# Row sums of an attention block moved from TensorE to VectorE, with three shared FFN banks in PSUM

## Chip, cores and metric

The kernel runs on one core of one Trainium2 chip. The metric is the device time of one execution in microseconds (us), median of several executions. An execution is slow when it lies over 1.5% above the fastest of its kernel. Differences of about 1 us between two kernels are near the noise: the 95% interval of a ratio is 0.2 to 0.7% wide on each side. The profile comes from one extra execution of each kernel. Its span is about 1.7 us shorter than the device time (before: 274.5 against 276.1 us).

## The reference

Block-sparse attention, then a multiplicative feed-forward network (FFN) without an activation:

```python
# q, k, v: (4 batches, 8 heads, 768 positions, 64), float32
scores = q @ k.T / 8                     # per batch and head
mask = same block or a neighbour, or first/last block on either side,
       or one of 3 sampled blocks        # blocks of 32; the same mask for every head
attn = exp(scores) / sum(exp(scores))    # over the unmasked keys
x = (attn @ v) as (3072 tokens, 512)
out = ((x @ w1) * (x @ w2)) @ w3 @ w_out # 512 -> 1024 -> 1024 -> 512, float32
```

## The kernel before

Everything on the chip is bfloat16 with float32 sums in PSUM. Scores are computed transposed (keys on partitions, queries along the free dimension), so that the weights `e` can be the moving operand of the value product. A sum over keys is then a sum over partitions, and TensorE makes it, with a matrix of ones as the stationary operand. `w3 @ w_out` is folded into one matrix `wf` on the chip, because nothing stands between the two.

The work: 4 batches x 3 query tiles of 256 x 2 sets of four heads = 24 groups. Each group has 3 pairs of key chunks (6 x 128 keys). One score unit is two heads of one pair: 4 score matmuls, one exp on ScalarE (1024 elements a partition), one mask multiplication on VectorE. One pair of four heads then goes through the value matmuls:

```python
def values(b, t, Q, kp):                 # one pair of key chunks, four heads
    def emit(eng):
        if kp == 0:
            acc["o"] = ps_o.tile([128, 512], F32, tag="o", name="o")
            acc["d"] = ps_o.tile([128, QT], F32, tag="d", name="d")   # own bank
        ...
        for k2 in range(2):
            kc = 2 * kp + k2
            first, last = kc == 0, kc == C - 1
            for part in range(3):        # parts 0, 1: two halves of v; part 2: ones
                for g in range(4):
                    ...
                    if part == 2:
                        nc.tensor.matmul(d[rows, :], lhsT=ones, rhs=rhs, start=first, ...)
                    else:
                        nc.tensor.matmul(o[rows, part * QT:(part + 1) * QT], lhsT=vn[...], rhs=rhs, ...)
```

Four matmuls with 32 output rows each (`g`) run side by side in the array: in the trace of this kernel they start 3 to 4 ns apart, and the next set of four 0.109 us after the set before it. So there are 1152 value matmuls and 576 matmuls with ones. After the third pair ScalarE makes 1/d as exp(-ln d), and VectorE writes `x = o * (1/d)`.

The kernel lays out PSUM in eight banks: four for two score tiles, one for `o`, one for `d`, two (`ps_f`) for everything else: FFN (`pa`, `pb`, `po`), the folding of the weights (`w3p`, `wp`) and the mask building.

The order of instructions is fixed when the program is built. A list scheduler ("planner") has an estimated duration for each operation. It places attention units (modes "qk", "pv") and takes FFN pieces (mode "f") as filler between them.

```python
# pick_pe, shortened
if rv is not None and rv <= near:                      # a value burst is ready
    op = self.pv[0]
    whole = all(o.ready() is not None and o.ready() <= rv + 0.3 for o in ...)
    if op.kp or (whole and self.mode == "qk") or rf is None or rf > near:
        return rv, self.pv
if rf is not None and rf <= near and self.due > 0.3:   # FFN owed: SHARE per score unit
    return rf, self.fill
...
```

The softmax here doesn't subtract the row's maximum and nothing guards it: scores larger than these inputs give would overflow.

## Time and profile before

| | before |
|---|---|
| device time | 276.1 us |
| PE, DVE, ACT busy | 97, 68, 66% of the span |
| PE's part of the chain of waits | 91% |
| last attention work (last `x`) ends | 243 us |
| last score matmul at half speed | about 20 us |

The page's busy table and the first two lines of the chain of waits (who the last instruction was waiting for, followed back to the start):

```profile
span 274.5 us, 7499 instructions
PE 265.9 (97%) x3228; PEld 135.1 (49%) x3228; DVE 186.5 (68%) x299; ACT 180.0 (66%) x241; POOL 63.0 (23%) x100
PE 91%; ACT 3%; DVE 3%; POOL 1%; issue 1%; POOLq 0%; ACTq 0%
PE pa L597 16%; PE pb L614 16%; PE po L635 16%; PE s L466 15%; PE o L508 13%; PE d L505 6%; PE wp L578 4%; ACT e L473 3%; PE tp L375 3%; PE mp L446 1%; DVE e L477 1%; PE w3p L561 1%; POOL A L257 0%; DVE wf_sb L284 0%; DVE qkt L284 0%
```

The sums (`d`, L505) are 6% of the chain. Groups of instructions by line and shape (lines that are left out are marked ...); after the first bar stand busy time and mean ns of one:

```profile
L477 DVE TENSOR_TENSOR e<-e,mask 128x1024 bf16<-128x1024 bf16 x144 | 98.5, 688 | 47.8 <-ACT e L473 46.6
...
L505 PE MATMUL d<-e,ones 128*32 128x256 bf16 x576 | 41.9, 277 | 0.0
```

Busy time of matmuls counts overlap once per group but not between groups, so 41.9 us is not what they cost. The start times say more. From the timeline of PE, columns start, length, line, tile, shape and count:

```profile
142.88 1.04 PE L597 MATMUL pa<-x,w_sb 128*128 128x512 bf16 x4
143.76 1.03 PE L614 MATMUL pb<-x,w_sb 128*128 128x512 bf16 x4
144.70 1.02 PE L597 MATMUL pa<-x,w_sb 128*128 128x512 bf16 x4
145.66 0.40 PE L508 MATMUL o<-e,vn 128*32 128x256 bf16 x8
145.88 0.28 PE L505 MATMUL d<-e,ones 128*32 128x256 bf16 x4
...
147.74 0.61 PE L466 MATMUL s<-qkt 64*128 64x256 bf16 x8
148.28 1.04 PE L614 MATMUL pb<-x,w_sb 128*128 128x512 bf16 x4
```

One burst of 72 value and sum matmuls takes 2.08 us (145.66 to 147.74), of which a third are sums.

```profile
1.21 3.17 PE L278 MATMUL warm<-warm_sb 128*128 128x512 bf16 x7 [1.21 <-DVE warm_sb L239]
...
13.15 0.61 PE L466 MATMUL s<-qkt 64*128 64x256 bf16 x4
...
22.44 0.39 PE L466 MATMUL s<-qkt 64*128 64x256 bf16 x4
```

Four score matmuls take 0.61 us at 13 us and 0.39 us at 22 us. The records of one engine overlap (`pa` matmuls last 0.38 us and start 0.22 us apart), so the distance from start to start is the better measure: matmuls of 512 columns start 0.43 us apart at the beginning (`warm`) and 0.22 us apart later (`pa`). So the array runs at half its later speed for the first 20 us, although PE is busy most of the time (9.5 of the 10 us from 10 to 20 us). The page's row of the granted clock shows 9 (90% or more) for these slices too, so only the matmuls tell: the trace holds no record of the clock before 20.8 us, and the row counts time without a record as full speed.

### The profile page before, as it was taken

The page shows a single profiled execution, that of the slowest core. Times are in us where ns is not written, and L with a number is a line of the kernel's source. Part 1 is how long each engine was busy: PE and PEld are TensorE (multiplying, and loading weights), DVE is VectorE, ACT ScalarE, POOL GpSimd, SP SyncE. Part 2 cuts the span into 40 slices and gives each one's busy share as a digit, 9 for nine tenths or more (in the row PEclk, how much of TensorE's full clock was granted, in tenths as well). Part 3 has the DMA queues.
Part 4 walks back from the last instruction along what each step waited for, and adds up shares of the span by engine and source line. Part 5 has one row for each costly group of instructions (what it writes and reads, how often), then busy time and mean ns, then how long its engine had stood idle before and what let it go on. Part 6 is the DMA issues. An engine that isn't in the chain of part 4 may idle for free.

```text
span 274.5 us, 7499 instructions
## 1 busy us (share of the span) xinstructions
PE 265.9 (97%) x3228; PEld 135.1 (49%) x3228; DVE 186.5 (68%) x299; ACT 180.0 (66%) x241; POOL 63.0 (23%) x100
## 2 busy tenths in 40 slices
PE   6999999899999999999999999999999999999994
PEld 2445555445554545545455544554554555444441
DVE  5576657767688677677755868666767656756752
ACT  4667669865557797595996679978868968520000
POOL 8635568944290000038510000000000000000000
PEclk9999999999999999999999999999999999999999
DMA  7999999999695051069993000300002100002003
GB/s 224 170 206 206 204 205 203 188 156 146 83 133 38 13 163 41 0 80 128 178 173 122 2 0 2 117 38 2 2 0 79 58 25 2 2 38 115 2 21 132
DMA packets 53734, 25.39 MB, mean 93 GB/s; under 512 B 39237, under 2 KB 48709, under 8 KB 53701
## 3 DMA queue, kind: packets, MB, share of 16 engines
q0 software_dynamic: 36176, 13.90, 43.2%
q1 hardware_dynamic: 17344, 10.88, 15.7%
q8 instruction: 25, 0.41, 0.6%
q10 hardware_dynamic: 180, 0.13, 0.1%
q14 instruction: 9, 0.07, 0.1%
HBM read 29.36 MB, written 6.29 MB: 130 GB/s over the span
## 4 chain that ended last, share of the span: by engine, by line
PE 91%; ACT 3%; DVE 3%; POOL 1%; issue 1%; POOLq 0%; ACTq 0%
PE pa L597 16%; PE pb L614 16%; PE po L635 16%; PE s L466 15%; PE o L508 13%; PE d L505 6%; PE wp L578 4%; ACT e L473 3%; PE tp L375 3%; PE mp L446 1%; DVE e L477 1%; PE w3p L561 1%; POOL A L257 0%; DVE wf_sb L284 0%; DVE qkt L284 0%
## 5 line engine op out<-in xcount | busy, mean ns | idle before, releaser
L473 ACT ACTIVATE e<-s 128x1024 bf16<-128x1024 f32 x144 | 141.4, 1028 | 31.4 <-PE s L466 31.3
L477 DVE TENSOR_TENSOR e<-e,mask 128x1024 bf16<-128x1024 bf16 x144 | 98.5, 688 | 47.8 <-ACT e L473 46.6
L508 PE MATMUL o<-e,vn 128*32 128x256 bf16 x1152 | 52.4, 278 | 0.8 <-DVE x L541 0.5
L466 PE MATMUL s<-qkt 64*128 64x256 bf16 x576 | 48.9, 279 | 1.4 <-ACT e L473 1.1
L597 PE MATMUL pa<-x,w_sb 128*128 128x512 bf16 x192 | 49.5, 380 | 0.0
L614 PE MATMUL pb<-x,w_sb 128*128 128x512 bf16 x192 | 49.4, 379 | 0.0
L635 PE MATMUL po<-wf_sb,h 128*128 128x512 bf16 x192 | 44.7, 380 | 0.0
L505 PE MATMUL d<-e,ones 128*32 128x256 bf16 x576 | 41.9, 277 | 0.0
L466 PEld LDWEIGHTS <-qkt 64*128 64x128 bf16 x576 | 22.1, 95 | 31.4 <-issue 26.8
L508 PEld LDWEIGHTS <-vn 128*32 128x32 bf16 x1152 | 27.8, 97 | 16.7 <-issue 15.5
L620 DVE TENSOR_TENSOR h<-pb,a 128x512 bf16<-128x512 f32 x48 | 33.0, 687 | 3.6 <-PE pb L614 2.6
L614 PEld LDWEIGHTS <-w_sb 128*128 128x128 bf16 x192 | 17.8, 97 | 23.5 <-issue 4.8
L635 PEld LDWEIGHTS <-h 128*128 128x128 bf16 x192 | 17.3, 98 | 22.3 <-issue 3.6
L597 PEld LDWEIGHTS <-w_sb 128*128 128x128 bf16 x192 | 16.3, 97 | 22.1 <-issue 6.5
L317 POOL DMA_DIRECT2D vn<-in_v_dram x16 | 11.5, 722 | 48.4 <-PE d L505 46.8
L284 DVE CAST a<-pa 128x512 bf16<-128x512 f32 x27 | 18.6, 688 | 5.6 <-PE pa L597 5.6
L532 ACT ACTIVATE ln<-d 128x256 f32<-128x256 f32 x24 | 9.2, 385 | 17.4 <-PE d L505 17.2
L643 ACT COPY ob<-po 128x256 f32<-128x256 f32 x1 | 0.4, 372 | 28.4 <-PE po L635 28.4
L541 DVE TENSOR_TENSOR x<-o,rec 128x512 bf16<-128x512 f32 x24 | 16.4, 685 | 2.6 <-ACT rec L536 2.5
L505 PEld LDWEIGHTS <-ones 128*32 128x32 bf16 x576 | 16.4, 98 | 0.5
L578 PE MATMUL wp<-wo_sb,w3t_sb 128*128 128x512 bf16 x64 | 16.5, 381 | 0.0
L284 ACT CAST a<-pa 128x512 bf16<-128x512 f32 x21 | 12.2, 582 | 5.7 <-PE pa L597 5.7
(56 smaller groups left out, 156.3 us busy)
## 6 DMA issues: line engine op xcount, KB each, us to landing
out_dram<-ob SPq DMA_DIRECT2D x23, 256.0 KB, 2.0
vn<-in_v_dram POOLq DMA_DIRECT2D x16, 192.0 KB, 5.9
w_sb<-in_moe_w_dram POOLq DMA_DIRECT2D x8, 256.0 KB, 10.2
w_sb<-in_moe_w_dram POOLq DMA_DIRECT2D x16, 128.0 KB, 5.4
nt<-in_q_dram POOLq DMA_DIRECT2D x16, 96.0 KB, 4.6
nt<-in_k_dram POOLq DMA_DIRECT2D x16, 96.0 KB, 4.8
qn<-in_q_dram POOLq DMA_DIRECT2D x6, 192.0 KB, 8.4
kn<-in_k_dram POOLq DMA_DIRECT2D x6, 192.0 KB, 8.4
```

Source lines behind the costliest of these rows:

```text
L284: (nc.scalar.copy if eng == "ACT" else nc.vector.tensor_copy)(dst, src)
L466: nc.tensor.matmul(s[:, h, k2 * QT:(k2 + 1) * QT], lhsT=qk[64 * h:64 * h + 64, 1, kc * 128:(kc + 1) * 128], rhs=qk[64 * h:64 * h + 64, 0, ...
L473: nc.scalar.activation(e, box["s"], AF.Exp, scale=1.0 / 8.0)
L477: nc.vector.tensor_tensor(e, e, mask[:, t, kp:kp + 1, :].to_broadcast((128, 2, 512)), op=ALU.mult)
L505: nc.tensor.matmul(d[rows, :], lhsT=ones, rhs=rhs, start=first, stop=last, skip_group_check=True)
L508: nc.tensor.matmul(o[rows, part * QT:(part + 1) * QT], lhsT=vn[b, 2 * Q + i][:, h, kc, 32 * part:32 * part + 32], rhs=rhs, start=first and ...
L541: nc.vector.tensor_tensor(X[i][:, 2 * Q:2 * Q + 2, half * QT:(half + 1) * QT], box["o"].rearrange("p (s n) -> p s n", s=2), box["rec"].to_ ...
L578: nc.tensor.matmul(box["p"], lhsT=w3t_sb[:, j, i * 128:(i + 1) * 128], rhs=wo_sb[:, j, :], start=j == 0, stop=j == NF - 1)
L597: nc.tensor.matmul(p, lhsT=w1_sb[:, c, f * 128:(f + 1) * 128], rhs=X[i][:, c, :], start=c == 0, stop=c == 3)
L614: nc.tensor.matmul(p, lhsT=w2_sb[:, c, f * 128:(f + 1) * 128], rhs=X[i][:, c, :], start=c == 0, stop=c == 3)
L620: nc.vector.tensor_tensor(box["h"][:, f, :], box["pb", f], box["a", f], op=ALU.mult)
L635: nc.tensor.matmul(box["o", n], lhsT=box["h"][:, f, n * 128:(n + 1) * 128], rhs=wf_sb[:, f, :], start=f == 0, stop=f == NF - 1)
```

## The change

The intent: `e` of one group is summed over its three pairs by VectorE (two elementwise adds of 2048 elements a partition), and TensorE multiplies only that sum with ones. That leaves 8 in place of 24 matmuls for each group. To make room on VectorE, the masks of four heads become one operation, which also skips the query columns that belong to the first or last block, where the mask is one everywhere (960 x 2 in place of 1024 x 2 elements). The sums no longer hold a bank of their own; the FFN pool gets a third bank, and sums take one of the three. Further: seven buffers of `e` for four heads in place of thirteen for two; transposes of q and k in two halves through the FFN pool, which ScalarE may copy out too; four w3 buffers in place of eight; new numbers in the planner; dummy matmuls in the planned gaps of TensorE before the first value product.

```diff
-    ps_f = pool("ps_f", 2, space=PSUM)
+    ps_f = pool("ps_f", 3, space=PSUM)
...
-    warm(7)
+    def warm(gap):
+        for _ in range(int(gap / 0.22)):
+            nc.tensor.matmul(spare[:, :256], lhsT=warm_sb[:, :128], rhs=warm_sb[:, :256], ...)
+    warm(3.1)
...  # in the planner, before the first value product: self.warm(start - self.free["PE"] - 0.2)
-    SHARE = 0.6
+    SHARE = 0.58
+    COLD = 6.0          # matmuls planned before 6 us count double
...
-            nc.vector.tensor_tensor(e, e, mask[:, t, kp:kp + 1, :].to_broadcast((128, 2, 512)),
-                                    op=ALU.mult)
+            e = E[key].rearrange("p g (c n) -> p g c n", c=4)[:, :, :, 4:124]
+            m = mask[:, t, kp:kp + 1, :].rearrange("p o (c n) -> p o c n", c=4)[:, :, :, 4:124]
+            nc.vector.tensor_tensor(e, e, m.to_broadcast((128, 4, 4, 120)), op=ALU.mult)
...
+        def add1(eng):
+            box["sum"] = dpool.tile([128, 4, 512], BF16, tag="sum", name="sum")
+            nc.vector.tensor_tensor(box["sum"], E[es[0]], E[es[1]], op=ALU.add)
+        def add2(eng):
+            nc.vector.tensor_tensor(box["sum"], box["sum"], E[es[2]], op=ALU.add)
...
+        def sums(eng):
+            d = acc["d"] = ps_f.tile([128, 512], F32, tag="f", name="d")
+            for k2 in range(2):
+                for g in range(4):
+                    nc.tensor.matmul(d[32 * g:32 * g + 32, :QT], lhsT=ones,
+                                     rhs=box["sum"][:, g, k2 * QT:(k2 + 1) * QT], start=k2 == 0, ...)
...
```

More of the change, by code (lines that the diff above doesn't have):

```diff
@@ L46, in __init__ @@
         self.mode, self.lat = mode, lat
+        self.after = 0.0
         self.end = None
@@ L54, in ready @@
                 return None
-            at = max(at, e)
+            at = max(at, e + self.after)
         for slots, _ in self.takes:
@@ L67, with __init__ @@
     PATIENCE = 0.2
-    SHARE = 0.6
-    def __init__(self, free):
+    SHARE = 0.58
+    COLD = 6.0
+    def __init__(self, free, warm):
         self.free = dict(free)
+        self.warm = warm
         self.side = {e: [] for e in self.free if e != "PE"}
@@ L84, in run_op @@
         if eng == "PE":
+            if op.mode == "pv":
+                self.warm = None
+            if self.warm:
+                self.warm(start - self.free[eng] - 0.2)
             if op.mode != self.mode:
@@ L94, in run_op @@
             slots.taken.append(hold)
-        self.free[eng] = start + op.dur
-        op.end = start + op.dur + op.lat
+        dur = op.dur
+        if eng == "PE" and start < self.COLD:
+            dur *= 2
+        self.free[eng] = start + dur
+        op.end = start + dur + op.lat
         op.emit(eng)
@@ L117, in pick_pe @@
             whole = all(o.ready() is not None and o.ready() <= rv + 0.3
-                        for o in list(self.pv)[1:3 - op.kp])
-            if op.kp or (whole and self.mode == "qk") or rf is None or rf > near:
+                        for o in list(self.pv)[1:1 + op.rest])
+            if not op.first or (whole and self.mode == "qk") or rf is None or rf > near:
                 return rv, self.pv
@@ L154, in go @@
             start, _, eng, op, q = best
+            start = max(self.free[eng], op.ready())
             if eng == "PE":
@@ L199 @@
     wts = pool("wts", 1)
+    w3pool = pool("w3pool", 4)
     nat = pool("nat", 4)
@@ L202 @@
     qkt = pool("qkt", 8)
-    epool = pool("epool", 13)
+    NE = 7
+    epool = pool("epool", NE)
+    dpool = pool("dpool", 2)
     small = pool("small", 2)
@@ L210 @@
     ps_o = pool("ps_o", 1, space=PSUM)
-    ps_f = pool("ps_f", 2, space=PSUM)
-    S_SLOTS, F_SLOTS, O_SLOTS = Slots(2), Slots(2), Slots(1)
-    E_SLOTS, X_SLOTS, A_SLOTS, H_SLOTS, T_SLOTS = Slots(13), Slots(3), Slots(4), Slots(2), Slots(8)
+    ps_f = pool("ps_f", 3, space=PSUM)
+    S_SLOTS, F_SLOTS, O_SLOTS = Slots(2), Slots(3), Slots(1)
+    E_SLOTS, D_SLOTS = Slots(NE), Slots(2)
+    X_SLOTS, A_SLOTS, H_SLOTS, T_SLOTS = Slots(3), Slots(4), Slots(2), Slots(8)
+    N_SLOTS, W_SLOTS = Slots(4), Slots(4)
     order = tc.manual_schedule(
@@ L272 @@
                                        in1=A, op0=ALU.is_equal, op1=ALU.max)
-    def warm(n):
-        w = ps_f.tile([128, 512], F32, tag="f", name="warm")
-        for _ in range(n):
-            nc.tensor.matmul(w, lhsT=warm_sb[:, :128], rhs=warm_sb, start=True, stop=True)
-    warm(7)
-    plan = Planner({"PE": 4.3, "ACT": 2.6, "DVE": 4.3, "POOL": 3.4, "SP": 3.0})
+    spare = ps_o.tile([128, 512], F32, tag="o", name="spare")
+    def warm(gap):
+        for _ in range(int(gap / 0.22)):
+            nc.tensor.matmul(spare[:, :256], lhsT=warm_sb[:, :128], rhs=warm_sb[:, :256],
+                             start=True, stop=True)
+    warm(3.1)
+    plan = Planner({"PE": 4.3, "ACT": 2.6, "DVE": 4.3, "POOL": 3.4, "SP": 3.0}, warm)
     def copy(eng, dst, src):
@@ L292, in load @@
     def load(emit, nbytes, deps=()):
-        op = plan.add(Op("POOL", 0.75, None, deps))
+        op = plan.add(Op("POOL", 0.75, None))
+        op.deps = deps
         def go(eng):
@@ L302 @@
     qn, kn, vn, landed = {}, {}, {}, {}
-    nat_users = {"q": [], "k": [], "v": [], "nt": []}
+    nat_users = {"q": [], "k": [], "v": []}
     def nat_slot(tag, n):
@@ L327 @@
     w2_sb = wts.tile([128, 4, d_ff], BF16, tag="w2")
-    w3_sb = wts.tile([128, NF, d_ff], BF16, tag="w3")
     w3t_sb = wts.tile([128, NF, d_ff], BF16, tag="w3t")
@@ L341, in load_w12, with emit @@
         return op
-    w3_in = {}
+    w3_in, w3_sb, w3_hold = {}, {}, {}
     def load_w3(lo, hi):
         for i in range(lo, hi):
-            w3_in[i] = load(lambda i=i: nc.gpsimd.dma_start(
-                out=w3_sb[:, i, :], in_=moe_w3[128 * i:128 * i + 128, :]), 128 * d_ff * 4)
+            def emit(i=i):
+                w3_sb[i] = w3pool.tile([128, d_ff], BF16, tag="w3", name="w3")
+                nc.gpsimd.dma_start(out=w3_sb[i], in_=moe_w3[128 * i:128 * i + 128, :])
+            w3_in[i] = load(emit, 128 * d_ff * 4)
+            w3_hold[i] = Hold()
+            w3_in[i].takes.append((W_SLOTS, w3_hold[i]))
     QK, QK_at, QK_hold = {}, {}, {}
@@ L367, in transposes, with emit @@
     def transposes(b, pr):
-        box = {}
-        def emit(eng):
-            tp = box["p"] = ps_s.tile([128, 2, 1024], BF16, tag="s", name="tp")
-            for x, src in ((0, qn[b, pr]), (1, kn[b, pr])):
+        hold = qk_hold(b, pr)
+        ops = []
+        for x, (tag, nat_of) in enumerate((("q", qn), ("k", kn))):
+            box = {}
+            def emit(eng, x=x, nat_of=nat_of, box=box):
+                tp = box["p"] = ps_f.tile([128, 1024], BF16, tag="f", name="tp")
                 for c in range(C):
@@ L374, in emit @@
                     for h in range(2):
-                        nc.tensor.transpose(tp[64 * h:64 * h + 64, x, c * 128:(c + 1) * 128],
-                                            src[:, h, c, :], ident)
-        ins = [landed["q", b, pr], landed["k", b, pr]]
-        hold = Hold()
-        op = Op("PE", 0.66, emit, ins, [(S_SLOTS, hold)], "t", lat=0.2)
-        for d in ins:
-            d.users.append(op)
-        def out_(eng):
-            t = QK[b, pr] = qkt.tile([128, 2, S], BF16, tag="qkt", name="qkt")
-            copy(eng, t, box["p"][:, :, :S])
@@ L386, in transposes, with out_ @@
-        hold.frees = QK_at[b, pr] = plan.add(Op("DVE", 0.9, out_, [op],
-                                                [(T_SLOTS, qk_hold(b, pr))]))
-        return op
+                        nc.tensor.transpose(tp[64 * h:64 * h + 64, c * 128:(c + 1) * 128],
+                                            nat_of[b, pr][:, h, c, :], ident)
+            src = landed[tag, b, pr]
+            op = Op("PE", 0.33, emit, [src], [(F_SLOTS, Hold())], "t", lat=0.2)
+            src.users.append(op)
+            def out_(eng, x=x, box=box):
+                if x == 0:
+                    QK[b, pr] = qkt.tile([128, 2, S], BF16, tag="qkt", name="qkt")
+                copy(eng, QK[b, pr][:, x, :], box["p"][:, :S])
@@ L390 @@
+            at = plan.add(Op(("DVE", "ACT"), 0.5, out_, [op] + ([QK_at[b, pr]] if x else []),
+                             [] if x else [(T_SLOTS, hold)]))
+            op.takes[0][1].frees = QK_at[b, pr] = at
+            ops.append(op)
+        return ops
+    MARGIN = 3.0
     qd, kd = (x.rearrange("b h (p c) d -> b p c h d", c=C) for x in (q, k))
     def turned(b, pr):
-        ns = {}
-        ops = []
-        deps = []
+        ns, ops, holds = {}, [], []
         for x, src in enumerate((qd, kd)):
-            mine, was = nat_slot("nt", 4)
+            hold = Hold()
+            holds.append(hold)
@@ L403, in emit @@
                     nc.gpsimd.dma_start(out=n[:, :, h, :], in_=src[b][:, :, 2 * pr + h, :])
-            ops.append(load(emit, 2 * 128 * 2 * C * D * 4, was))
-            deps.append(mine)
+            op = load(emit, 2 * 128 * 2 * C * D * 4)
+            op.takes.append((N_SLOTS, hold))
+            ops.append(op)
         load_one(b, pr, "v")
         def turn(eng):
+            dma_at[0] += 4.0
             t = QK[b, pr] = qkt.tile([128, 2, S], BF16, tag="qkt", name="qkt")
@@ L412, in turn @@
                                             in_=ns[x].rearrange("p c h d -> p (c h d)"))
-        op = QK_at[b, pr] = plan.add(Op("SP", 0.9, turn, ops + [QK_at[b - 1, o] for o in range(4)],
-                                        [(T_SLOTS, qk_hold(b, pr))], lat=4.0))
-        for mine in deps:
-            mine.append(op)
+        op = QK_at[b, pr] = plan.add(Op("SP", 2.5, turn,
+                                        ops + [QK_at[b - 1, o] for o in range(4)],
+                                        [(T_SLOTS, qk_hold(b, pr))], lat=2.5))
+        op.after = MARGIN
+        for hold in holds:
+            hold.frees = op
     hot2 = hot.rearrange("e c p -> e (c p)")
@@ L451, in build_mask @@
         return op
-    E, E_at, E_hold = {}, {}, {}
+    E, E_at, E_hold, exps = {}, {}, {}, {}
     def scores(b, t, Q, kp, i):
         box = {}
-        key = (b, t, Q, kp, i)
+        key = (b, t, Q, kp)
         def emit(eng):
@@ L471, in exp @@
         def exp(eng):
-            e = E[key] = epool.tile([128, 2, 512], BF16, tag="e", name="e")
-            nc.scalar.activation(e, box["s"], AF.Exp, scale=1.0 / 8.0)
+            if key not in E:
+                E[key] = epool.tile([128, 4, 512], BF16, tag="e", name="e")
+            nc.scalar.activation(E[key][:, 2 * i:2 * i + 2, :], box["s"], AF.Exp, scale=1.0 / 8.0)
         def keep(eng):
-            e = E[key]
-            nc.vector.tensor_tensor(e, e, mask[:, t, kp:kp + 1, :].to_broadcast((128, 2, 512)),
-                                    op=ALU.mult)
+            e = E[key].rearrange("p g (c n) -> p g c n", c=4)[:, :, :, 4:124]
+            m = mask[:, t, kp:kp + 1, :].rearrange("p o (c n) -> p o c n", c=4)[:, :, :, 4:124]
+            nc.vector.tensor_tensor(e, e, m.to_broadcast((128, 4, 4, 120)), op=ALU.mult)
         hold = Hold()
-        E_hold[key] = Hold()
         op = Op("PE", 0.22, emit, [QK_at[b, 2 * Q + i]], [(S_SLOTS, hold)], "qk", lat=0.2)
-        hold.frees = plan.add(Op("ACT", 0.97, exp, [op], [(E_SLOTS, E_hold[key])]))
-        E_at[key] = plan.add(Op("DVE", 0.62, keep, [hold.frees, mask_at[t, kp]]))
+        takes = []
+        if key not in exps:
+            E_hold[key] = Hold()
+            takes.append((E_SLOTS, E_hold[key]))
+        hold.frees = plan.add(Op("ACT", 0.97, exp, [op] + exps.get(key, []), takes))
+        exps.setdefault(key, []).append(hold.frees)
+        if len(exps[key]) == 2:
+            E_at[key] = plan.add(Op("DVE", 1.09, keep, exps[key] + [mask_at[t, kp]]))
         QK_hold[b, 2 * Q + i].frees = op
@@ L487, with values, product, emit @@
     acc = {}
-    def values(b, t, Q, kp):
-        def emit(eng):
-            if kp == 0:
-                acc["o"] = ps_o.tile([128, 512], F32, tag="o", name="o")
-                acc["d"] = ps_o.tile([128, QT], F32, tag="d", name="d")
-            o, d = acc["o"], acc["d"]
-            es = [E.pop((b, t, Q, kp, i)) for i in range(2)]
-            for k2 in range(2):
-                kc = 2 * kp + k2
-                first, last = kc == 0, kc == C - 1
-                for part in range(3):
-                    for g in range(4):
-                        i, h = divmod(g, 2)
-                        rhs = es[i][:, h, k2 * QT:(k2 + 1) * QT]
-                        rows = slice(32 * g, 32 * g + 32)
-                        if part == 2:
-                            nc.tensor.matmul(d[rows, :], lhsT=ones, rhs=rhs, start=first,
-                                             stop=last, skip_group_check=True)
-                        else:
-                            nc.tensor.matmul(o[rows, part * QT:(part + 1) * QT],
+    def values(b, t, Q):
+        box = {}
+        es = [(b, t, Q, kp) for kp in range(3)]
+        ins = [landed["v", b, 2 * Q + i] for i in range(2)]
+        d_hold = Hold()
+        def add1(eng):
[3 more added lines that the diff above has]
+            nc.vector.tensor_tensor(box["sum"], box["sum"], E[es[2]], op=ALU.add)
+        sum1 = plan.add(Op("DVE", 1.16, add1, [E_at[es[0]], E_at[es[1]]], [(D_SLOTS, d_hold)]))
+        sum2 = plan.add(Op("DVE", 1.16, add2, [sum1, E_at[es[2]]]))
+        def product(kp):
+            def emit(eng):
+                if kp == 0:
+                    acc["o"] = ps_o.tile([128, 512], F32, tag="o", name="o")
+                e = E[es[kp]]
+                for k2 in range(2):
+                    kc = 2 * kp + k2
+                    for part in range(2):
+                        for g in range(4):
+                            i, h = divmod(g, 2)
+                            nc.tensor.matmul(acc["o"][32 * g:32 * g + 32, part * QT:(part + 1) * QT],
@@ L509, in emit @@
                                              lhsT=vn[b, 2 * Q + i][:, h, kc,
                                                                    32 * part:32 * part + 32],
-                                             rhs=rhs, start=first and part == 0, stop=last,
+                                             rhs=e[:, g, k2 * QT:(k2 + 1) * QT],
+                                             start=kc == 0 and part == 0, stop=kc == C - 1,
                                              skip_group_check=True)
-        ins = [landed["v", b, 2 * Q + i] for i in range(2)]
@@ L514, in values @@
-        op = Op("PE", 0.65, emit, [E_at[b, t, Q, kp, i] for i in range(2)] + ins,
-                [(O_SLOTS, Hold())] if kp == 0 else (), "pv", lat=0.2)
-        for i in range(2):
-            E_hold[b, t, Q, kp, i].frees = op
-        for d in ins:
-            d.users.append(op)
-        op.kp = kp
-        return op
+            return emit
+        def sums(eng):
+            d = acc["d"] = ps_f.tile([128, 512], F32, tag="f", name="d")
+            for k2 in range(2):
+                for g in range(4):
+                    nc.tensor.matmul(d[32 * g:32 * g + 32, :QT], lhsT=ones,
+                                     rhs=box["sum"][:, g, k2 * QT:(k2 + 1) * QT], start=k2 == 0,
+                                     stop=k2 == 1, skip_group_check=True)
@@ new lines, in values @@
+        o_hold = Hold()
+        ops = []
+        for kp in range(3):
+            op = Op("PE", 0.43, product(kp), [E_at[es[kp]]] + ins,
+                    [(O_SLOTS, o_hold)] if kp == 0 else (), "pv", lat=0.2)
+            op.rest, op.first = 3 - kp, kp == 0
+            ops.append(op)
+        E_hold[es[0]].frees, E_hold[es[1]].frees = ops[0], ops[1]
+        E_hold[es[2]].frees = ops[2]
+        for d in ins:
+            d.users.append(ops[2])
+        f_hold = Hold()
+        op = Op("PE", 0.22, sums, [sum2], [(F_SLOTS, f_hold)], "pv", lat=0.2)
@@ L523, with normalize @@
+        op.rest, op.first = 0, False
+        ops.append(op)
+        d_hold.frees = op
+        plan.pv.extend(ops)
+        normalize(b, t, Q, o_hold, f_hold, op)
     X, X_at, X_hold = {}, {}, {}
-    def normalize(b, t, Q, first, last):
+    def normalize(b, t, Q, o_hold, f_hold, last):
         i, half = divmod(b * NT + t, 2)
@@ L531, in ln_ @@
             box["ln"] = small.tile([128, QT], F32, tag="ln", name="ln")
-            nc.scalar.activation(box["ln"], box["d"], AF.Ln)
+            nc.scalar.activation(box["ln"], box["d"][:, :QT], AF.Ln)
         def rec_(eng):
@@ L544, in x_ @@
                 box["rec"].to_broadcast((128, 2, QT)), op=ALU.mult)
-        ln = plan.add(Op("ACT", 0.34, ln_, [last]))
+        ln = f_hold.frees = plan.add(Op("ACT", 0.34, ln_, [last]))
         rec = plan.add(Op("ACT", 0.36, rec_, [ln]))
@@ L550, in normalize @@
             takes = [(X_SLOTS, X_hold[i])]
-        x_op = first.takes[0][1].frees = plan.add(Op("DVE", 0.62, x_, [rec], takes))
+        x_op = o_hold.frees = plan.add(Op("DVE", 0.62, x_, [rec], takes))
         X_at.setdefault(i, []).append(x_op)
@@ L561, in emit @@
                 nc.tensor.transpose(tp[:, j, :],
-                                    w3_sb[:, i, (4 * jh + j) * 128:(4 * jh + j + 1) * 128], ident)
+                                    w3_sb[i][:, (4 * jh + j) * 128:(4 * jh + j + 1) * 128], ident)
         op, hold = f_op(0.23, emit, [w3_in[i]])
+        w3_hold[i].frees = op
         hold.frees = either(0.42, lambda eng: copy(
@@ L720 @@
                 turned(b + 1, pr)
-        plan.qk.extend(at.get(n, ()))
+        for ops in at.get(n, ()):
+            plan.qk.extend(ops)
         plan.qk.append(scores(*g, i))
-        if n % 2 == 1 or n == 2:
-            pass
-    for n, g in enumerate(groups):
-        b, t, Q, kp = g
-        plan.pv.append(values(*g))
-        if kp == 2:
-            normalize(b, t, Q, plan.pv[-3], plan.pv[-1])
-            while nx < NX and len(X_at.get(nx, ())) == 4:
-                ffn(nx)
-                nx += 1
+    for b, t, Q, kp in groups[::3]:
+        values(b, t, Q)
+        while nx < NX and len(X_at.get(nx, ())) == 4:
+            ffn(nx)
+            nx += 1
     plan.go()
```

## The prediction

> **What bounds the kernel now.** TensorE. The page's busy table gives PE 97% of the 274.5 us span, DVE 68%, ACT 66%; the chain of waits is 91% PE. Busy by stretches: PE idle is 8.6 us in all, 4.9 us of it before 60 us and 3.7 us at the end, after the last matmul. Attention ends at 242 us; then PE runs FFN alone.
>
> A second loss hides in "busy": the timeline shows every matmul at half speed until about 20.4 us (four score matmuls 0.61 us, later 0.39). [...]
>
> **Removed.** Row sums: 576 matmuls (L505) become 192. In the timeline a whole burst of 72 matmuls runs from 102.28 to 104.36 us: 0.029 us each, 0.116 per four. The 384 removed are worth 384 x 0.027 to 0.029 = 10.4 to 11.1 us. The chain of waits has L505 at 5.7% of the span, so all of it is on PE's path.
>
> **Startup.** Dummy matmuls fill PE's gaps until the first value product. If that frees the clock at about 6 us instead of 20.4, the 13 us of cold work becomes 6.5. But exp, mask copies and loads then set the pace, so I count 3.5 us.
>
> **Added.** DVE: 144 masks (0.69 us long, 0.61 from start to start when back to back) become 72 of 1920 elements, and 48 adds of 2048 elements come in. [...] DVE goes from 186 to about 220 us busy, as some copies move to ACT (180 to about 190). From 10 to 232 us both would be near 86 to 88% (now about 75%). That leaves less slack: I allow 2.5 us of new PE stalls on s, o and f banks. The longer chain add, sum, ln, exp, x (about 2.5 us more) matters little with 10 us per group.
>
> **Moved.** Sums and transposes take FFN banks, now three. Halving the w3 buffers makes the in-order load queue wait for w3 transposes, which could delay w1, w2 and the first FFN tile (first pa at 64.7 us).
>
> **Sum.** 276.05 - 10.6 (sums) - 3.5 (clock) + 2.5 (stalls) = 264.4 us, rounded to 264; range 257 to 270.5. Faster by over 2%: 0.87; within 2%: 0.10; slower: 0.03.
>
> **What would show it.** Row-sum matmuls 192, their busy near 14 us; adds near 1.2 us, masks near 1.15 us; DVE busy 215 to 230 us; PE still 94 to 97% busy and over 85% of the chain; score matmuls at full speed from 6 to 10 us; attention ending near 230 us, first pa near 60 us.
>
> **What would make it wrong.** [...] DVE and ACT together too full, so that PE waits for masks and bank copies (PE below 92%: 268 to 275). Loads late after the w3 wait, leaving PE idle at 40 to 65 us. The other way: a startup gain of all 6.5 us and no new stalls: 257 to 259.

The sum came to 276.05 - 10.6 - 3.5 + 2.5 = 264.4 us. Two steps stand as the author's guesses, which the trace of before did not show: that dummy matmuls end the stretch at half speed (behind the 3.5 us), and the durations that gave 45 us more of masks and adds (behind "about 220 us" of VectorE, together with the copies that move to ACT).

## The result

The changed kernel takes 262.24 us (median of 4; 261.74 to 262.64), the kernel before 276.1 us: a ratio of 0.951 (95% interval 0.947 to 0.955), 13.9 us less. Ratios here are the mean time of one kernel's fast runs over that of the other's of the same rounds, so not quite the ratio of the quoted medians. The predicted 264.0 us was close, but the sum behind it was not right in every term, as the experiments show.

The page after:

```profile
span 260.9 us, 6636 instructions
PE 248.4 (95%) x2819; PEld 127.6 (49%) x2852; DVE 212.3 (81%) x250; ACT 198.8 (76%) x274; POOL 62.7 (24%) x100
PE 86%; DVE 5%; ACT 3%; DMA 2%; issue 2%; SPq 1%
PE pb L678 17%; PE po L699 16%; PE pa L661 16%; PE s L496 14%; PE o L552 13%; PE wp L642 4%; DMA raw<-in_k_dram 2%; DVE e L509 2%; PE d L564 2%; PE tp L399 2%; ACT e L504 2%; PE mp L476 1%; DVE x L604 1%; PE w3p L624 1%; SPq L251 1%
```

TensorE is still the bound; the sums fell from 6% to 2% of the chain. VectorE went up by 26 us, ScalarE by 19 us (copies that VectorE no longer had time for). Of the matmuls 33 records are missing (2852 weight loads, 2819 matmuls), so sums over matmuls below come from traces without gaps. The groups that answer to those of before:

```profile
L509 DVE TENSOR_TENSOR e<-e,mask 128x1920 bf16<-128x1920 bf16 x72 | 82.9, 1154 | 16.7 <-ACT e L504 15.7
...
L535 DVE TENSOR_TENSOR sum<-e 128x2048 bf16<-128x2048 bf16 x24 | 29.3, 1222 | 0.7
L538 DVE TENSOR_TENSOR sum<-sum,e 128x2048 bf16<-128x2048 bf16 x24 | 29.3, 1222 | 0.5
...
L564 PE MATMUL d<-sum,ones 128*32 128x256 bf16 x192 | 9.5, 274 | 0.4 <-DVE sum L538 0.4
```

The adds took 1222 ns for 2048 elements. The strided 120-element runs of the mask kept the same rate: 1154 ns for 1920. Against the 688 ns for 1024 elements before, both take 0.52 ns more for each element more.

A burst, in the timeline of PE:

```profile
150.15 0.61 PE L496 MATMUL s<-qkt 64*128 64x256 bf16 x8
150.69 1.50 PE L552 MATMUL o<-e,vn 128*32 128x256 bf16 x48
152.01 0.39 PE L564 MATMUL d<-sum,ones 128*32 128x256 bf16 x8
152.33 1.04 PE L661 MATMUL pa<-x,w_sb 128*128 128x512 bf16 x3
```

It takes 1.64 us (150.69 to 152.33) for a whole group, against 2.08 us: 0.44 us, times 24 groups 10.6 us. And the start:

```profile
1.21 3.17 PE L295 MATMUL spare<-warm_sb 128*128 128x256 bf16 x14 [1.21 <-DVE warm_sb L255]
...
13.66 0.61 PE L496 MATMUL s<-qkt 64*128 64x256 bf16 x4
...
14.52 0.39 PE L295 MATMUL spare<-warm_sb 128*128 128x256 bf16 x1
...
19.28 1.03 PE L496 MATMUL s<-qkt 64*128 64x256 bf16 x8
```

Only one dummy matmul was placed after the opening ones, and score matmuls are as slow at 19 us as before (eight in 1.03 us). So the 3.5 us that the prediction booked for an earlier clock cannot have come from there in this execution. Something else paid.

### The profile page after: what moved, and what is told of

Read it like the earlier page. It is cut to its first block, busy times and chain, and to the rows that moved or that the text cites. A ratio compares the mean times of both kernels' runs of the same rounds, so it can differ in the third digit from the quotient of the medians.

```text
span 260.9 us, 6636 instructions
## 1 busy us (share of the span) xinstructions
PE 248.4 (95%) x2819; PEld 127.6 (49%) x2852; DVE 212.3 (81%) x250; ACT 198.8 (76%) x274; POOL 62.7 (24%) x100
## 4 chain that ended last, share of the span: by engine, by line
PE 86%; DVE 5%; ACT 3%; DMA 2%; issue 2%; SPq 1%
PE pb L678 17%; PE po L699 16%; PE pa L661 16%; PE s L496 14%; PE o L552 13%; PE wp L642 4%; DMA raw<-in_k_dram 2%; DVE e L509 2%; PE d L564 2%; PE tp L399 2%; ACT e L504 2%; PE mp L476 1%; DVE x L604 1%; PE w3p L624 1%; SPq L251 1%
## 5 line engine op out<-in xcount | busy, mean ns | idle before, releaser
L509 DVE TENSOR_TENSOR e<-e,mask 128x1920 bf16<-128x1920 bf16 x72 | 82.9, 1154 | 16.7 <-ACT e L504 15.7
L661 PE MATMUL pa<-x,w_sb 128*128 128x512 bf16 x175 | 47.6, 380 | 2.6 <-DVE x L604 1.3
L496 PE MATMUL s<-qkt 64*128 64x256 bf16 x576 | 46.9, 279 | 0.7 <-ACT e L504 0.5
L699 PE MATMUL po<-wf_sb,h 128*128 128x512 bf16 x186 | 43.4, 380 | 0.7 <-issue 0.6
L552 PE MATMUL o<-e,vn 128*32 128x256 bf16 x1152 | 38.0, 278 | 1.2 <-DVE x L604 1.0
L496 PEld LDWEIGHTS <-qkt 64*128 64x128 bf16 x576 | 22.5, 96 | 30.7 <-issue 27.8
L535 DVE TENSOR_TENSOR sum<-e 128x2048 bf16<-128x2048 bf16 x24 | 29.3, 1222 | 0.7
L538 DVE TENSOR_TENSOR sum<-sum,e 128x2048 bf16<-128x2048 bf16 x24 | 29.3, 1222 | 0.5
L661 PEld LDWEIGHTS <-w_sb 128*128 128x128 bf16 x192 | 16.7, 98 | 23.2 <-issue 6.7
L302 ACT CAST a<-pa 128x512 bf16<-128x512 f32 x36 | 21.2, 588 | 2.4 <-PE pa L661 1.5
L429 POOL DMA_DIRECT2D nt<-in_q_dram x16 | 13.2, 830 | 22.4 <-DMA qkt<-nt 14.6
L336 POOL DMA_DIRECT2D vn<-in_v_dram x16 | 11.6, 727 | 24.2 <-PE o L552 20.4
L642 PE MATMUL wp<-wo_sb,w3t_sb 128*128 128x512 bf16 x56 | 15.6, 380 | 0.7 <-issue 0.5
```

The costliest lines, as they stand in the source:

```text
L302: (nc.scalar.copy if eng == "ACT" else nc.vector.tensor_copy)(dst, src)
L496: nc.tensor.matmul(s[:, h, k2 * QT:(k2 + 1) * QT], lhsT=qk[64 * h:64 * h + 64, 1, kc * 128:(kc + 1) * 128], rhs=qk[64 * h:64 * h + 64, 0, ...
L509: nc.vector.tensor_tensor(e, e, m.to_broadcast((128, 4, 4, 120)), op=ALU.mult)
L535: nc.vector.tensor_tensor(box["sum"], E[es[0]], E[es[1]], op=ALU.add)
L538: nc.vector.tensor_tensor(box["sum"], box["sum"], E[es[2]], op=ALU.add)
L552: nc.tensor.matmul(acc["o"][32 * g:32 * g + 32, part * QT:(part + 1) * QT], lhsT=vn[b, 2 * Q + i][:, h, kc, 32 * part:32 * part + 32], rhs ...
```

## Experiments

Theory A: the gain is the 384 matmuls that left TensorE's path, less some new stalls. Rival B: the gain comes mainly from the third FFN bank and the new plan. Each run is compared with the kernel before in the same rounds (its median was 275.8 to 276.1 us); all results were correct.

| run | what differs | us | ratio to before |
|---|---|---|---|
| changed kernel | | 262.2 | 0.951 |
| e1_pe_sums | changed, sums by TensorE | 270.4 | 0.979 |
| e7_one_add | changed, one add of two | 264.2 | 0.954 |
| e9_adds_old_banks | changed, PSUM as before | 268.9 | 0.975 |
| e2_two_banks | changed, two FFN banks | 282.9 | 1.020 |
| e8_before_three_banks | before, three FFN banks | 271.7 | 0.984 |
| e6_extra_add | changed, 18 adds more | 263.7 | 0.956 |
| e4_split_masks | changed, most masks split | 266.1 | 0.965 |
| e5_old_plan | changed, most old planner numbers | 262.5 | 0.952 |
| e11_share_half | changed, SHARE 0.5 | 262.8 | 0.953 |
| e3_long_warm | changed, 31 dummies at the start | 263.6 | 0.955 |
| e10_dense_warm | changed, dummies all through the start | 265.6 | 0.963 |
| e12_last_group | changed, one planner condition | 261.3 | 0.947 |

### The sums back on TensorE: e1_pe_sums

```diff
-        def add1 ... add2 ... sums          # no adds on VectorE
+        acc["d"] = ps_f.tile(...)           # with "o", at the first pair
+                    for g in range(4):      # in every chunk, as in the kernel before
+                        nc.tensor.matmul(acc["d"][...], lhsT=ones, rhs=e[:, g, ...], start=kc == 0, ...)
```

> The changed kernel with the row sums put back on TensorE (576 ones matmuls, inside the product bursts as in the kernel before; no adds on VectorE; the sums sit in one of the three FFN banks). Theory A (the gain is mainly the 384 matmuls taken off the PE path): 262.2 + 10.5 us, less up to 2 us because VectorE has 55 us less to do: 270.5 to 273. Rival B (the gain comes mainly from the third FFN bank and the new plan, the adds only pay for themselves): 263 to 267.

Measured: 270.4 us, 0.1 us below the range of A, far from B. With all else as changed, moving the sums is worth 8.1 us by the medians (7.6 us by the ratios, 0.979 against 0.951). That is about the prediction's -10.6 + 2.5. But 5.7 us of the 13.9 have nothing to do with the sums.

### The third bank: e8_before_three_banks, e2_two_banks, e9_adds_old_banks

In the kernel before, alone:

```diff
-    ps_f = pool("ps_f", 2, space=PSUM)
+    ps_f = pool("ps_f", 3, space=PSUM)
-                acc["d"] = ps_o.tile([128, QT], F32, tag="d", name="d")
+                acc["d"] = ps_f.tile([128, 512], F32, tag="f", name="d")[:, :QT]
```

> The kernel before, with the row sums moved into the FFN pool, which gets a third bank; nothing else. If the bank is worth 3 us by itself: 272 to 274. Rival B: 266 to 270. If the bank only helps together with the shorter bursts, since here the sums hold a bank through a whole burst: 275 to 276.5.

Measured: 271.7 us, 4.4 us less (ratio 0.981 to 0.986), slightly better than expected. Sharing the sums' bank is a gain by itself. My reading: `d` needs its bank for a short time in each group, and the FFN can use it for the rest.

In the changed kernel, the other way round:

```diff
-    ps_f = pool("ps_f", 3, space=PSUM)
+    ps_f = pool("ps_f", 2, space=PSUM)
-            d = acc["d"] = ps_f.tile([128, 512], F32, tag="f", name="d")
+            d = acc["d"] = ps_o.tile([128, 512], F32, tag="d", name="d")
```

> The changed kernel with two FFN banks again and the row sums in a bank of their own; adds, merged masks and plan as changed. In the trace the FFN, fold and mask matmuls together took 158.9 us from start to start before and 155.3 after, so I expect the third bank to be worth about 3 us: 264.5 to 266. Rival B: 268 to 272. If the third bank is worth nothing: 262 to 263.

Measured: 282.9 us (279.5 to 285.3; the last is a slow execution, and the three fast ones have a median of 282.2), by the fast ones 1.3 to 2.7% slower than the kernel before and outside all expectations. The timeline of e2_two_banks shows why; in brackets stands the idle time before a row and what ended it:

```profile
83.82 7.07 PE L699 MATMUL po<-wf_sb,h 128*128 128x512 bf16 x32
...
91.83 0.39 PE L496 MATMUL s<-qkt 64*128 64x256 bf16 x4
...
92.26 1.02 ACT L504 ACTIVATE e<-s 128x1024 bf16<-128x1024 f32 x1 [15.96 <-PE s L496]
...
96.53 1.66 POOL L429 DMA_DIRECT2D nt<-in_q_dram  x2 [29.81 <-issue]
```

The transposes stand in the same queue as the scores and now need an FFN bank. With two banks the planner gave both to FFN pieces up to 91 us; scores behind the transposes waited, ScalarE had nothing for 16 us, and the loads of the next batch started late. The loss went on: TensorE was busy for 8.0 and 7.3 of 10 us, and the granted clock fell to 0.85 and 0.64 (windows; the columns are the stretch, its length, busy time of PE, PEld, DVE, ACT and POOL with counts, then granted clock, DMA share and GB/s):

```profile
90.00:100.00 10.00, 8.00 (x129) 4.07 (x126) 7.70 (x9) 6.96 (x8) 3.47 (x5) 0.85 0.82 145
100.00:110.00 10.00, 7.32 (x92) 4.08 (x89) 7.28 (x8) 7.79 (x12) 6.11 (x8) 0.64 1.76 147
```

So this run tests the new dependence of transposes on FFN banks, not the third bank. A cleaner run puts the PSUM use of before back as a whole:

```diff
     (as in e2_two_banks, and)
-                tp = box["p"] = ps_f.tile([128, 1024], BF16, tag="f", name="tp")     # halves
+            tp = box["p"] = ps_s.tile([128, 2, 1024], BF16, tag="s", name="tp")      # whole, as before
```

> The changed kernel with the PSUM use of before as a whole: two FFN banks, sums in a bank of their own, transposes in one piece in the score banks; adds and merged masks kept. The run with two banks alone lost 20 us because transposes waited for an FFN bank at the head of the score queue, so it did not test the third bank. If adds and bank are two separate gains (8.1 us and 4.4 us in the runs so far) this is 276.1 - 8.1 - 1.3 = 266.7: 265.5 to 268. If the adds only pay with the third bank: 270 to 275. If the bank is worth nothing beside the adds: 262 to 264.

Measured: 268.9 us, 1 us outside the range for two separate gains, on the high side. Together the four kernels make a table of two by two:

| | PSUM as before | three FFN banks |
|---|---|---|
| TensorE sums everything | 276.1 (before) | 270.4 (e1) |
| VectorE adds first | 268.9 (e9) | 262.2 (changed) |

The adds are worth 7.2 us in the left column and 8.1 us in the right, the banks 5.7 and 6.7 us. They are two nearly independent gains; at most 1 us comes from having both, which is within the noise. (The corners of the left column also differ in the masks, the w3 buffers and the planner's numbers, so the left figure of the adds is less clean than the right one.)

How does a bank save time on an engine that was 97% busy? The smaller part is waits inside FFN work. In the lines of before, `pa` to `pb` takes 0.88 us (142.88 to 143.76), but `pb` to the next `pa` 0.94 us (143.76 to 144.70). I read this as a wait for a bank: the median of such steps from 25 us on is 0.94 us in e9 with two FFN banks and 0.87 us in e11_share_half with three.

The larger part is in the order. I counted how often TensorE goes from one kind of work (scores, values and sums, FFN and folding, transposes; mask building and dummies as kinds of their own) to another, by the weight loads of each trace, of which no record is missing: 218 bursts before, 187 in e8, 187 in e1, 210 in the changed kernel, 251 in e9. With a free bank more often at hand, the planner lets FFN pieces follow each other. Time is lost at the changes of kind, as follows. Four traces have no missing record (before, e9, e10_dense_warm and e11_share_half). In before and e11 I took the time from the last matmul of a burst to the first of the next, less the usual pitch: 0.137 us on average in the first and 0.144 in the second, waits included (from 25 us on). That pitch is a mean in which matmuls that run side by side start 3 to 4 ns apart, so the figure is on the high side. Counting 0.109 us for each set of four value matmuls or two score matmuls (the usual distance from set to set) leaves 0.12 to 0.13 us. I use 0.12 to 0.137. So e8 has 31 bursts less, an estimate of 3.7 to 4.2 us; 4.4 us were measured. From e9 to the changed kernel it is 41 bursts less, or 37 without the dummies, 4.4 to 5.1 us; 6.7 us were measured.

Two of the complete traces, e9 and e11 (the changed kernel but for SHARE), can be split directly. From 25 us to its last matmul TensorE takes 237.1 us in e9 and 232.0 in e11; at the usual pitches the matmuls account for 207 us in both. The rest is 30.1 and 25.1 us: inside FFN bursts 3.8 and 2.0 us, everywhere else, mostly at the changes of kind (220 and 187 of them), 26.4 and 23.2 us. So of 5.0 us, 1.8 are waits inside FFN work and 3.2 go with the changes. This is arithmetic that fits, not an experiment that changes the number of bursts alone, and it doesn't tell how much of the time at a change is a wait for data or a bank.

### Half of the adds: e7_one_add

```diff
-            nc.vector.tensor_tensor(box["sum"], box["sum"], E[es[2]], op=ALU.add)     # add2 gone
+            for n, src in enumerate((box["sum"], E[es[2]])):                          # 16 ones matmuls
```

> The changed kernel with one add in place of two: VectorE adds the weights of two chunk pairs, TensorE sums that sum and the third pair (384 ones matmuls). Theory A: 192 matmuls more at 0.027 us = +5.2 us, less about 1 us of relief for VectorE: 265.5 to 267.5. If VectorE had become a second bound, the relief of 28 us there would pay for it: 260 to 263.

Measured: 264.2 us, so the 192 matmuls that came back cost 1.9 us, not 5.2, and the first add is worth 6.2 us, the second 1.9 (0.9 by the ratios, 0.954 against 0.951, whose intervals overlap). No theory named this range. With one add less, more groups go through in one burst: 193 bursts in place of 210, and no group's sums in a burst of their own, where the changed kernel has 7 of 24. At 0.12 to 0.137 us, 17 bursts would account for 2.0 to 2.3 of the missing 3.3 us; this is not shown by a run of its own.

### VectorE's slack: e6_extra_add, e4_split_masks

```diff
+        if b:                               # batches 1 to 3: the first add a second time
+            sum1 = plan.add(Op("DVE", 1.16, again, [sum1]))
```

> The changed kernel with the first add done twice in batches 1 to 3 (18 adds more, 18 x 1.14 = 20.5 us more on VectorE; results unchanged). If VectorE still has slack: 262 to 265. If it had become a second bound: 270 or more.

Measured: 263.7 us. VectorE's busy time rose from 212.3 to 228.4 us, and the time by 1.5 us (intervals of the ratios: 0.947 to 0.955 and 0.954 to 0.958). VectorE is not a second bound; at 81% it has slack. (The first attempts of this run and of the next, in all batches, could not be built: the planner blocked itself over the banks of the weight folding. So both leave batch 0 alone.)

```diff
+        if b:                               # batches 1 to 3: one mask operation for two heads
+            E_at[key] = plan.add(Op("DVE", 0.59, keep, [hold.frees, mask_at[t, kp]] + ...))
```

> The changed kernel with the masks of batches 1 to 3 in two operations of 960 elements each, as before in count (126 mask operations in place of 72). VectorE's busy time rises by about 54 x 0.077 to 0.15 = 4 to 8 us. If TensorE is the bound and VectorE has slack: 262 to 263. If merging the masks was needed to make room for the adds: 264 to 267.

Measured: 266.1 us, 3.8 us more for 5.8 us of added VectorE time (218.1 us busy; 0.11 us for each of the 54 operations more). By the expectation this says that merging the masks was needed to make room. The run above contradicts that: nearly three times the added busy time (16.1 us), in larger pieces, cost less. In the trace of e4 `pa` waits 2.1 us for `x` in all, against 1.3 in the changed kernel, and `s` 2.3 us for exp against 0.5. Why splitting masks would lead there stays open, so the slack of VectorE is shown for adds and not for small pieces; the number of bursts (208) does not explain it.

### The planner's numbers: e5_old_plan, e11_share_half

```diff
-    SHARE = 0.58
+    SHARE = 0.6
-    MARGIN = 3.0          # after the DMA transposes
+    MARGIN = 0.0
     (also their old durations, and no dummy matmuls in gaps)
```

> The changed kernel with the planner's old numbers (0.6 us of FFN owed per score unit in place of 0.58, no margin after the DMA transposes, their old durations, no dummy matmuls in gaps). Theory A: within 1.5 us of the changed kernel, 261.5 to 264. If the new plan's numbers carry a good part of the gain: 265 to 270.

> The changed kernel with one number of the planner changed (0.5 us of FFN owed per score unit in place of 0.58), to see how far the order alone moves the time: if plans differ by chance by 1 to 2 us, 261 to 264.5; if the plan is a lever of its own, beyond that.

Measured: 262.5 and 262.8 us. The new numbers carry none of the gain that can be seen, and these two changes of the order move the time by some tenths (e4 shows that an order can cost 3.8 us). (COLD could not be taken back: without it the planner blocks itself.) Since e5 also places no dummy matmul in a gap, that part of the change does nothing that can be seen either.

### The cold clock: e3_long_warm, e10_dense_warm

```diff
-    warm(3.1)
+    warm(6.9)             # 31 dummy matmuls in place of 14; PE planned from 7.9 us
```

> The changed kernel with 31 dummy matmuls before the start in place of 14 (about 6.6 us at half speed[...]); the planner is told that TensorE is free at 7.9 us. If a long enough unbroken burst frees the clock: matmuls at full speed from about 5 to 8 us (four score matmuls under 0.4 us) in place of about 20. Theory C (the cold clock costs at most little, as exp, masks and loads set the pace at the start): 261 to 263.5, the delay of 3 us and the gain cancel. Theory D (it costs the full 6.5 us): 258 to 260. If the clock falls back or isn't freed: 264 to 266.

Measured: 263.6 us (261.99 to 264.48), 0.1 us above the range of C, in two pairs of executions (see below). The trace tells more than the time:

```profile
1.20 5.38 PE L295 MATMUL spare<-warm_sb 128*128 128x256 bf16 x31 [1.20 <-DVE ones L257]
...
9.87 0.39 PE L476 MATMUL mp<-G,hot 24*128 24x256 bf16 x2 [2.08 <-DVE G L302]
10.19 0.39 PE L496 MATMUL s<-qkt 64*128 64x256 bf16 x4
...
12.88 0.61 PE L496 MATMUL s<-qkt 64*128 64x256 bf16 x4
```

The dummies go from 0.21 to 0.11 us apart at 5.0 us, after 3.8 us without a break. Full speed was lost again between 11.6 and 12.0 us (two `mp` matmuls take 0.39 us at 11.3 and 0.60 us at 12.0), although no gap before that was longer than 2.08 us.

But a longer burst is not what makes the difference alone. Twelve traces open with the 3.2 us of dummies. In nine of them (before and changed kernel among them) the matmuls stayed at half speed after it; in three, e1, e2 and e11, they were at full speed by 4.9 us. From e11:

```profile
1.20 3.17 PE L295 MATMUL spare<-warm_sb 128*128 128x256 bf16 x14 [1.20 <-DVE warm_sb L255]
...
4.98 0.53 PE L399 MATMUL tp<-ident,qn 128*64 128x128 bf16 x12
...
6.96 0.39 PE L496 MATMUL s<-qkt 64*128 64x256 bf16 x4
...
10.66 1.04 PE L496 MATMUL s<-qkt 64*128 64x256 bf16 x8
```

There it was lost again at 8.0 us by the trace's clock record. So after the same opening the clock was free in some of these executions and not in others. The second step was to keep it:

```diff
+    warm(5.3)             # 24 dummies
-                self.warm(start - self.free[eng] - 0.2)
+                self.warm(2.05 * max(0.0, start - self.free[eng] - 0.2) + 0.45)   # and two before each operation
+                start += 0.22
```

> The changed kernel with 24 dummy matmuls at the start (to about 5.6 us) and two more, with gaps filled at full-speed pitch, before each TensorE operation until the first value product. The run with 31 at the start freed the clock at 4.8 us and lost it again at 11.7 us, after a gap of 2 us. Here it should be free from about 5 us and stay so. If the cold clock costs what the prediction counted (3.5 us): 258 to 260. If exp, masks and loads set the pace at the start and the clock costs nothing: 261.5 to 263.5. If the clock falls back: above 262.

Measured: 265.6 us. The clock, free from 5.0 us on, stayed free:

```profile
9.21 0.39 PE L497 MATMUL s<-qkt 64*128 64x256 bf16 x4 [0.84 <-DVE qkt L303]
9.54 0.39 PE L296 MATMUL spare<-warm_sb 128*128 128x256 bf16 x2
...
14.53 0.39 PE L497 MATMUL s<-qkt 64*128 64x256 bf16 x4
```

But the dummies ate it. By the start times (e10 and e11 have no missing record) dummies took 10.9 us in place of 3.6 in e11, 7.3 us more, while transposes, masks, scores, values and w3 transposes together took about 5 us less. (e11's own clock was free from 4.5 to 8.0 us, so against a start that is slow throughout the difference would be somewhat larger.) So a free clock is worth about 5 us of TensorE's time at the start, but bought with dummy matmuls it costs more. What a clock free through the whole start would be worth for nothing stays open; no run had it.

The record holds a hint. The mean granted clock of an execution tells how long the clock fell back after it had first come free: 0.973 in e11's trace is 13.65 us at half speed, 0.980 in e3's is 10.24 us, by the clock records. In e3 the two executions at 0.980 took 262.0 and 262.9 us, the two at 0.974 took 264.3 and 264.5. In the kernel before, two at 0.981 took 274.7 and 275.0 us, three at 0.974 or 0.975 took 276.0 to 276.6. So 3.4 us less at half speed went with 1.4 to 2.0 us less time, which would speak against Theory C. On the other hand, executions at 0.997 or more, which by the traces did not come free before 19 us, were no slower than those at 0.974 (kernel before: 275.5 to 276.5 us). These are few executions and no experiment; what the clock is worth at which moment stays open.

### The last group of attention: e12_last_group

The chain of waits of the changed kernel, near the end of attention (start, length, engine, tile):

```profile
226.56 6.69 PE po L699 x31
...
233.40 1.50 PE o L552 x48
234.90 0.25 PE d L564 x8
235.16 0.39 ACT ln L595
235.58 0.42 ACT rec L599
236.03 0.70 DVE x L604
236.77 0.59 PE pa L661 x2
```

The last value burst waits behind 6.7 us of FFN work, then the last FFN tile waits for `x` with nothing left to fill in. The condition `whole and self.mode == "qk"` cannot hold once the scores are used up and other work has followed the last of them.

```diff
-            if not op.first or (whole and self.mode == "qk") or rf is None or rf > near:
+            if not op.first or (whole and (self.mode == "qk" or not self.qk)) or rf is None or rf > near:
```

> The changed kernel with one condition of the planner mended: a value burst may start only right after a score unit, and once the scores are used up no burst could start before the FFN queue ran dry, so the last burst waited behind 6.9 us of FFN work and the last FFN tile then waited 1.3 us for x. With the condition lifted when no scores are left, only the order of the last 30 us differs. Expected: the last burst about 5 us earlier (at 228 to 230 us in place of 233.4), no wait of pa for x, and 1.0 to 1.5 us less: 260.5 to 261.3. If the tail is set by something else: 262.2.

Measured: 261.3 us, ratio 0.947 to the kernel before; the interval, 0.944 to 0.949, overlaps that of the changed kernel, which did not run in these rounds. The trace shows the mechanism as expected, the span being 259.5 in place of 260.9 us:

```profile
226.53 1.73 PE po L699 x8
228.25 1.43 PE o L552 x48
...
230.05 5.13 PE po L699 x23
235.18 0.86 PE pa L661 x4
```

## Why the prediction was right

The time was right (264 predicted, 262.2 measured) and the bound was right. Of the terms, one held, one failed, and one was missing. The failed and the missing one were of like size and opposite sign, so that the total came this close was luck.

- **Sums, -10.6 us, with stalls, +2.5 us: held.** A group's burst is 0.44 us shorter, 10.6 us over 24 groups, and e1 against the changed kernel gives 8.1 us net. The complete traces of before and e11 say the same of the removed work: at the usual pitches the matmuls after 25 us account for 217.6 and 206.9 us, 10.7 us less, and the rest of TensorE's time there for 27.8 and 25.1 us. The nature of the 2.5 us was not as put. I expected TensorE to wait for masks and banks; e6 shows that VectorE has slack. The changed kernel has 210 bursts to e1's 187, because the sums come later than the products: 7 of its 24 groups have their sums in a burst of their own, in e1 none. 23 x 0.12 to 0.137 = 2.8 to 3.2 us is an estimate by the same arithmetic.
- **Clock, -3.5 us: failed.** The step was "If that frees the clock at about 6 us instead of 20.4". It did not: in the profiled execution score matmuls were slow until about 20 us, one dummy was placed in a gap, and without any in the gaps (e5) the time is the same. Where the clock was free early, after the opening dummies (e11, at 4.5 us), it was lost again at 8.0 us. In the place of -3.5 us stand 0 us.
- **The third bank: missing from the sum.** The prediction names it ("FFN banks, now three") and gives it no number. e8 measures 4.4 us for it alone. This made up for the clock. Another 1.3 us (e8 to e1) goes to masks, transposes in halves, w3 buffers and plan together and was not taken apart.
- **VectorE's durations: held.** 1.22 and 1.15 us, where the signs had near 1.2 and near 1.15; back to back, the adds start 1.14 us apart and the masks 1.07. VectorE came to 212 us (about 220 predicted, and the sign said 215 to 230), ScalarE to 199 (190): more copies moved than I thought.
- **Signs:** PE 95% busy and 86% of the chain, as put. First `pa` at 61.8 us ("near 60"). The last `x` ended at 236.7 us, not near 230, in part by the planner condition that e12 mends. Busy time of the sums was 9.5 us, not 14: I scaled a number that holds overlap. Full-speed scores from 6 to 10 us: wrong.
- **Late loads after the w3 wait**, a named risk, hardly showed: from 40 to 60 us PE was idle 1.2 us before and 1.4 us in e11_share_half, whose trace is complete and whose loads wait in the same way.

## What to carry to other kernels

When one engine bounds a kernel, moving a reduction from it to one with slack can pay most of the price of the removed instructions: here 8.1 of 10.6 us, though the second half of the move brought only 1 to 2. Check afterwards how often the bound engine changes its kind of work, since results that come later can cut bursts in two. Cost every resource that a change frees, as a bank in PSUM, like an operation: here it was a third of the gain and stood in the prediction as a side remark. When a predicted time comes out right, still look for each term in the trace: two errors of 4 us had cancelled.
